# Reordering the first loads of an attention kernel, and moving its bias row out of the head

## The chip, the cores and the metric

One core of one Trainium2 chip. The metric is the device time of one execution in microseconds (us). The span of a profile, first to last instruction, is about 1.8 us shorter than the time of the same execution. In the profiles PE is TensorE (matmuls, and transposes as matmuls), DVE is VectorE; loads are issued from SP, ACT and POOL. Full and half clock mean the share of TensorE's clock that the profile records as granted.

## The reference

```python
x = A_x                                           # [1, 2048, 512] bf16
xn = layernorm(x)                                 # over 512
q = (xn @ wq) as 32 heads of 128
p = softmax(q k^T * 128**-0.5)                    # k_cache, v_cache: 32 heads, 2048 keys, 128
s = (p v) @ wo
h = relu(xn @ w1 + b1)**2                         # 512 -> 1792
g = silu(h @ w2 + b2)
out = x + s * g
```

## The kernel before

Five programs are written in one order and meet through semaphores. The query rows go through in four blocks of 512, and in each block through 32 heads. Nearly all the time is a steady loop of scores, exponentials and products, with the projections and the dense branch as side jobs in two further PSUM banks. The change concerns the head of the program: the loads of the first four x tiles, of the first head's keys (in two halves, transposed on TensorE) and of the bias row b1.

```python
    warm_up(36)                      # 36 matmuls on zeros, emitted first on TensorE
    ...
    ln_load(0, 0, SP)                # first x tile
    ln_load(0, 1, AC)                # second x tile, on ACT's queue
    load_k0(0)                       # first half of head 0's keys, SP
    fill_wq(0, AC)                   # head 0's query weights
    load_k0(1)                       # second half of the keys, SP
    ...
    k0_transpose(0); k0_copy(0)      # TensorE, then ACT
    ln_bn(0, 0); ln_rstd(0, 0, eng=DV)
    ln_bn(0, 1)
    ln_scale(0, 0)
    first_transpose(0)               # x tile 0, TensorE
    k0_transpose(1); k0_copy(1)
    ...
    first_copy(0); first_proj(0)
    bias_rows()                      # b1 transposed on TensorE
    ln_scale(0, 1)
    first_evac(0)
    bias_copy()
    first_transpose(1)
    gen_scores(0)
    ...
    second_proj(3)
    second_evac()
    t_bankF[:] = [t_q0[3], tok_xT[0][3]]   # the side banks are free
    gen_pv(3)
```

Each line emits on one engine, so an engine works in this order. The load of b1 is POOL's first DMA in this version.

The softmax here doesn't subtract the row's maximum and nothing guards it: scores larger than these inputs give would overflow.

## Time and profile before

| | kernel before |
|---|---|
| time, first three runs | 1237.77 us median (1237.75 to 1237.85) |
| span of the profile | 1236.3 us (that execution took 1238.05) |
| TensorE busy | 1231.7 us |
| first x tile landed | 3.68 us after the start of the span; the first statistics, which wait for it, start at 3.71, the prediction's figure |
| first scores start | 7.96 us |

The view of DMA issues for the first 0.9 us (tile, queue, count, size, us from issue to landing) gives the two x tiles that were issued at 0.72 (ACT) and 0.73 (SP):

```profile
x_ln<-in_A_x_dram ACTq DMA_DIRECT2D x1, 128.0 KB, 2.7
x_ln<-in_A_x_dram SPq DMA_DIRECT2D x1, 128.0 KB, 3.0
```

The reader is to see that both land within 0.3 us of each other.

### The profile page before, as it was taken

The page shows a single profiled execution, that of the slowest core. Times are in us where ns is not written, and L with a number is a line of the kernel's source. Part 1 is how long each engine was busy: PE and PEld are TensorE (multiplying, and loading weights), DVE is VectorE, ACT ScalarE, POOL GpSimd, SP SyncE. Part 2 cuts the span into 40 slices and gives each one's busy share as a digit, 9 for nine tenths or more (in the row PEclk, how much of TensorE's full clock was granted, in tenths as well). Part 3 has the DMA queues.
Part 4 walks back from the last instruction along what each step waited for, and adds up shares of the span by engine and source line. Part 5 has one row for each costly group of instructions (what it writes and reads, how often), then busy time and mean ns, then how long its engine had stood idle before and what let it go on. Part 6 is the DMA issues. An engine that isn't in the chain of part 4 may idle for free.

```text
span 1236.3 us, 26934 instructions
## 1 busy us (share of the span) xinstructions
PE 1231.7 (100%) x11885; PEld 818.8 (66%) x11885; DVE 472.8 (38%) x953; ACT 1053.5 (85%) x1044; POOL 31.9 (3%) x73
## 2 busy tenths in 40 slices
PE   9999999999999999999999999999999999999999
PEld 7666666666666666666666666666666666666665
DVE  4453323244435332334444532333344333324333
ACT  7888888888888888888888888888888888888885
POOL 1010000000002000000000200000000000000000
PEclk9999999999999999999999999999999999999999
DMA  9999998777879897778778878787788789878771
GB/s 211 203 231 209 185 178 134 130 144 143 139 152 172 141 161 129 139 139 145 133 133 170 172 138 143 141 148 134 133 146 148 146 154 158 137 134 146 145 123 31
DMA packets 686868, 185.41 MB, mean 150 GB/s; under 512 B 673536, under 2 KB 685568, under 8 KB 686752
## 3 DMA queue, kind: packets, MB, share of 16 engines
q1 hardware_dynamic: 684656, 179.62, 80.4%
q0 software_dynamic: 1424, 3.81, 1.2%
q8 instruction: 94, 1.54, 0.6%
q10 hardware_dynamic: 672, 0.26, 0.1%
q14 instruction: 22, 0.18, 0.1%
HBM read 96.60 MB, written 2.10 MB: 80 GB/s over the span
## 4 chain that ended last, share of the span: by engine, by line
PE 99%; DMA 0%; DVE 0%; issue 0%; SPq 0%; DVEq 0%
PE psO L157 38%; PE psA L152 36%; PE psF L152 25%; DMA kT<-in_A_k_cache_dram 0%; PE psA L157 0%; DVE out_t L165 0%; PE psF L196 0%; DVE tmp_t L175 0%; PE psO L196 0%; PE psO L152 0%; DVE xnT L179 0%; SPq L208 0%; PE psA L196 0%; DVEq L119 0%
## 5 line engine op out<-in xcount | busy, mean ns | idle before, releaser
L161 ACT ACTIVATE pT<-psA 128x1024 bf16<-128x1024 f32 x1024 | 1043.5, 1023 | 163.5 <-PE psA L152 118.1
L157 PEld LDWEIGHTS psO<-v_sb,pT 128*128 128x128 bf16 x8192 | 547.7, 98 | 240.5 <-issue 12.5
L157 PE MATMUL psO<-v_sb,pT 128*128 128x129 bf16 x8192 | 631.6, 220 | 0.0
L152 PE MATMUL psA<-qt_sb,kT 128*128 128x512 bf16 x2032 | 604.8, 379 | 0.0
L179 DVE COPY o_un<-psO 128x258 f32<-128x258 f32 x256 | 97.4, 422 | 399.4 <-PE psO L157 398.7
L152 PE MATMUL psF<-xnT,wq_sb 128*128 128x512 bf16 (+1 forms) x520 | 168.9, 374 | 0.2 <-DVE xnT L179 0.2
L152 PE MATMUL psF<-wo_all,oT 128*128 128x512 bf16 x480 | 163.8, 379 | 0.0
L152 PEld LDWEIGHTS psA<-qt_sb,kT 128*128 128x128 bf16 x2032 | 156.9, 98 | 0.0
L179 DVE CAST qt_sb<-psF 128x512 bf16<-128x512 f32 (+1 forms) x130 | 88.0, 677 | 97.4 <-PE psF L152 97.4
L165 DVE TENSOR_TENSOR o_bf<-o_un,rden 128x512 bf16<-128x512 f32 x128 | 88.6, 692 | 4.7 <-DVE rden L183 0.3
L152 PEld LDWEIGHTS psF<-xnT,wq_sb 128*128 128x128 bf16 x520 | 50.2, 98 | 60.1 <-issue 0.3
L171 DVE TENSOR_SCALAR r_t<-psF,b1f 128x512 bf16<-128x512 f32 x56 | 42.0, 750 | 117.5 <-PE psF L152 117.5
L152 PEld LDWEIGHTS psF<-wo_all,oT 128*128 128x128 bf16 x480 | 46.9, 98 | 56.4
L152 PE MATMUL psF<-xnT,w_sb 128*128 128x512 bf16 x224 | 77.1, 379 | 0.0
L152 PE MATMUL psF<-w_sb,h2T 128*128 128x512 bf16 x224 | 74.2, 379 | 0.0
L152 PEld LDWEIGHTS psF<-xnT,w_sb 128*128 128x128 bf16 x224 | 21.9, 98 | 26.5
L152 PEld LDWEIGHTS psF<-w_sb,h2T 128*128 128x128 bf16 x224 | 21.9, 98 | 26.5
L165 DVE TENSOR_TENSOR z_t<-psF,b2bc 128x512 f32<-128x512 f32 x16 | 11.1, 692 | 67.2 <-PE psF L152 67.2
L165 DVE TENSOR_TENSOR acc<-psF,acc 128x512 f32<-128x512 f32 x28 | 19.3, 689 | 29.9 <-PE psF L152 29.9
L208 POOL DMA_DIRECT2D out_dram<-out_t x12 | 6.7, 554 | 891.0 <-DVE out_t L165 891.0
L165 DVE TENSOR_TENSOR h2T<-r_t 128x512 bf16<-128x512 bf16 x56 | 23.8, 425 | 1.9
L183 DVE RECIPROCAL rden<-o_un 128x4 f32<-128x4 f32 x128 | 22.9, 179 | 4.4
(47 smaller groups left out, 165.6 us busy)
## 6 DMA issues: line engine op xcount, KB each, us to landing
v_sb<-in_A_v_cache_dram SPq DMA_DIRECT2D x127, 512.0 KB, 4.7
wq_sb<-in_A_wq_dram SPq DMA_DIRECT2D x127, 128.0 KB, 3.1
wo_all<-in_A_wo_dram SPq DMA_DIRECT2D x4, 1024.0 KB, 6.7
w_sb<-in_B_w_dram SPq DMA_DIRECT2D x14, 256.0 KB, 4.3
oT<-o_bf SPq DMA_TRANSPOSE x128, 4.0
x_t<-in_A_x_dram POOLq DMA_DIRECT2D x16, 128.0 KB, 3.4
kT<-in_A_k_cache_dram SPq DMA_TRANSPOSE x127, 4.5
x_ln<-in_A_x_dram SPq DMA_DIRECT2D x15, 128.0 KB, 3.8
```

The costliest lines, as they stand in the source:

```text
L152: return e.matmul(out, lhsT, rhs, start=start, stop=stop)
L157: return e.matmul(out, lhsT, rhs, start=start, stop=stop, skip_group_check=True)
L161: return e.activation(out, in_, func, bias=bias, scale=scale)
L165: return e.tensor_tensor(out, in0, in1, op)
L171: return e.tensor_scalar(out, in0, scalar1=scalar1, scalar2=scalar2, op0=op0, op1=op1)
L179: return e.tensor_copy(out, in_)
L183: return e.reciprocal(out, in_)
L208: return e.dma_start(out, in_)
```

## The change

It puts the first x tile alone at the head of SP's queue and the first half of the keys at the head of ACT's, so that both paths to the first scores start at once. It also takes the bias row out of the head: loaded from POOL later, transposed behind the last of the first projections, in a side bank instead of the scores' bank.

```diff
-    tok_b1 = S.emit_dma(GP, ...B_b1...)            # at the head of POOL's program
 ...
-                                 ... out=psA[:, 1536:1600]... deps=[tok_b1, t_ident])
+                                 ... out=bankF(1)[:, 0:64]... deps=[tok_b1, t_ident, tok_xT[0][TPB - 1]])
 ...
-                      deps=[t_k0[b], t_q0[qt], t_exp[pi - 2] if pi >= 2 else t_b1[0]],
+                      deps=[t_k0[b], t_q0[qt], t_exp[pi - 2] if pi >= 2 else None],
 ...
-    bank_no = [1]
+    bank_no = [0]
 ...
     ln_load(0, 0, SP)
-    ln_load(0, 1, AC)
-    load_k0(0)
+    ln_load(0, 1)
+    load_k0(0, AC)
     fill_wq(0, AC)
     load_k0(1)
 ...
     ln_rstd(0, 1, eng=DV)
+    tok_b1 = S.emit_dma(GP, ...B_b1...)
     first_copy(0)
     first_proj(0)
-    bias_rows()
     ln_scale(0, 1)
     first_evac(0)
-    bias_copy()
 ...
     second_evac()
-    t_bankF[:] = [t_q0[3], tok_xT[0][3]]
+    bias_rows()
+    bias_copy()
+    t_bankF[:] = [t_q0[3], t_b1[0]]
```

More of the change, by code (lines that the diff above doesn't have):

```diff
@@ L333, in bass_recurrent_scan__mha_block_cached__dense_activation_squared_relu__prompt_kernel @@
         t_ones = E(GP, partial(_memset, out=v_sb[:, i, :, Dh:Dh + 1], val=1.0))
-    tok_b1 = S.emit_dma(GP, partial(_dma, out=b1b[:], in_=B_b1.rearrange("(c p) -> c p", p=P)),
-                        sl_b1)
     t_xl = {}
@@ L394, in bass_recurrent_scan__mha_block_cached__dense_activation_squared_relu__prompt_kernel, with load_k0 @@
     t_xT = [None] * TPB
-    def load_k0(b):
+    def load_k0(b, eng=SP):
         n = NKT // 2
         t_k0[b] = S.emit_dma(
-            SP, partial(_dma, out=kT[:, NSL - 1, b * n * P:(b + 1) * n * P],
+            eng, partial(_dma, out=kT[:, NSL - 1, b * n * P:(b + 1) * n * P],
                         in_=A_k_cache[0, 0].rearrange("(p t) d -> p (t d)",
@@ L444, in bias_rows @@
     def bias_rows():
-        t_b1[0] = E(PE, partial(_peT, out=psA[:, 1536:1600].bitcast(BF16)[:, 0:NFC], in_=b1b[:],
-                                ident=ident[0:NFC, 0:NFC]), deps=[tok_b1, t_ident])
+        t_b1[0] = E(PE, partial(_peT, out=bankF(1)[:, 0:64].bitcast(BF16)[:, 0:NFC], in_=b1b[:],
+                                ident=ident[0:NFC, 0:NFC]), deps=[tok_b1, t_ident, tok_xT[0][TPB - 1]])
     def bias_copy():
         t_b1[0] = E(DV, partial(_copy, out=b1f[:],
-                                in_=psA[:, 1536:1600].bitcast(BF16)[:, 0:NFC]), deps=[t_b1[0]])
+                                in_=bankF(1)[:, 0:64].bitcast(BF16)[:, 0:NFC]), deps=[t_b1[0]])
     def first_proj(i):
@@ L913, in bass_recurrent_scan__mha_block_cached__dense_activation_squared_relu__prompt_kernel @@
     ln_rstd(0, 1, eng=DV)
+    tok_b1 = S.emit_dma(GP, partial(_dma, out=b1b[:], in_=B_b1.rearrange("(c p) -> c p", p=P)),
+                        sl_b1)
     first_copy(0)
     first_proj(0)
-    bias_rows()
     ln_scale(0, 1)
     first_evac(0)
-    bias_copy()
     first_transpose(1)
```

## The prediction

> **What bounds the kernel now.** I read the page first: the busy totals, then the chain of work that ended last, then the releasers of the costliest groups.
>
> ```profile
> PE 1231.7 (100%) x11885; PEld 818.8 (66%) x11885; DVE 472.8 (38%) x953; ACT 1053.5 (85%) x1044; POOL 31.9 (3%) x73
> PE 99%; DMA 0%; DVE 0%; issue 0%; SPq 0%; DVEq 0%
> L157 PE MATMUL psO<-v_sb,pT 128*128 128x129 bf16 x8192 | 631.6, 220 | 0.0
> L152 PE MATMUL psA<-qt_sb,kT 128*128 128x512 bf16 x2032 | 604.8, 379 | 0.0
> ```
>
> TensorE is busy for 1231.7 of the 1236.3 us of the span, it makes 99% of the chain, and both large matmul groups show 0.0 us of idle time before them. So only 4.6 us of TensorE's idle time exist in the whole execution. The change touches the start alone. The question is therefore how much earlier TensorE enters its unbroken stretch, and whether the start hands on a delay. I took the chain of waits restricted to the first 18 us, in order of time:
>
> ```profile
> 0.66 0.07 issue
> 0.73 0.40 SPq L208
> 1.12 0.06 issue
> 1.18 4.02 DMA kT<-in_A_k_cache_dram
> 5.20 0.05 issue
> 5.24 0.94 PE psO L196 x8
> 6.19 0.24 PE psF L196 x4
> 6.43 0.02 issue
> 6.45 0.43 DVE xnT L179
> 6.89 0.14 issue
> 7.02 0.38 PE psF L152 x4
> 7.41 0.11 PE psA L196
> 7.51 0.33 PE psF L196 x4
> 7.85 0.11 issue
> 7.96 1.05 PE psA L157 x16
> ```
>
> The reader is to see that the chain starts with the first half of the first head's keys (issued at 1.18, landed at 5.20), goes over their eight transposes, then over the first x tile's transposes, copy and projection, and reaches the first scores at 7.96. From there the same view is TensorE nearly without a break (one copy into xnT at 11.02 in between), up to 1232. So **the start of the first scores, 7.96, is the figure to predict**; the rest should follow it one for one.
>
> The chain names the keys, but the timeline of the first 8 us shows a second path that is nearly as long:
>
> ```profile
> 3.71 0.69 DVE L200 BATCH_NORM_STATS2 st_t<-x_ln 128x6 f32<-128x512 bf16 x1 [3.71 <-DMA x_ln<-in_A_x_dram]
> 4.72 0.68 DVE L200 BATCH_NORM_STATS2 st_t<-x_ln 128x6 f32<-128x512 bf16 x1
> 5.50 0.41 DVE L171 TENSOR_SCALAR xn_t<-x_ln,mv_t,rstd 128x512 bf16<-128x512 bf16 x1
> ```
>
> The first x tile lands at 3.71; statistics, aggregation, reciprocal root on POOL and scaling end at 5.50 + 0.41 = 5.91. Its TensorE transposes started at 6.03, when the key transposes ahead of them in TensorE's program were over. The key path therefore holds the x path back by about 0.1 us only (6.03 - 5.91, less the handing on of a semaphore). This is the number that caps what earlier keys can be worth.
>
> **What the Trainium skill says.** "DMA: Bandwidth & Descriptors", section "Issuing engines are not separate DMA queues": transfers issued from several engines run on the same 16 DMA engines and interleave, and issuing from two saves only the sequencer's issue time. The section "Queues, rings and completion order" of the same page adds that each DMA engine goes round between its queues packet by packet. The trace agrees on the sharing: between 2.2 and 2.8 us ACT's queue moved 0.09 MB and SP's 0.08 MB, both being 1024 B packets. It also shows something the sections do not say: from 1.6 to 2.2 us only ACT's queue moves anything (23 packets), though the two first loads were issued at 0.72 and 0.73. SP's first packet starts at 2.24 in the trace, ACT's at 1.76. "Trace Analysis", section "Summary: the profiler window per engine type", says that the row of such a DMA covers its issue and hides the data movement; so I use landings (0.73 + 3.0 and 0.72 + 2.7 in the view of DMA issues), not the 0.40 us rows.
>
> **The change part by part.**
>
> 1. The first half of the keys moves from second place on SP's queue (issue 1.18) to the head of ACT's (0.72). It gains 0.46 us of issue and no longer queues behind an x tile. It should start near 1.8 and has at least half of the engines: 256 KB at about two thirds of the 340 GB/s that the DMA view shows from 2.4 us on is some 1.2 us, so I estimate a landing at 3.6 to 3.9 instead of 5.20. On the path: 0.1 us, as above, because the x path stands behind it.
> 2. The second x tile moves from the head of ACT's queue to second on SP's. Landing now 0.72 + 2.7 = 3.4; then an estimated 4.0 to 4.4. VectorE wants it at 4.72, so 0.3 to 0.7 us of slack remain. On the path: 0.
> 3. The first x tile stays at the head of SP's queue, at the same issue time, but its company changes: before, 1024 B packets of the other x tile; then, 2048 B packets of keys. The mean packet times in the trace are 46 ns and 84 ns. Taking turns, x gets 1024 B each 46 + 84 = 130 ns on each of 16 engines, 126 GB/s, where it had 1024 B each 92 ns, 178 GB/s. Its 128 KB last 1.04 instead of 0.74 us at those rates, so up to 0.3 us later if ACT's queue starts first again. If instead SP starts first, x runs alone for about 0.5 us and lands up to 0.4 us earlier. This goes one for one into 7.96: between -0.4 and +0.25, and I put the mean at -0.05.
> 4. The second half of the keys and ACT's first weights: the total bytes are the same. I estimate keys at 5.0 (5.98 now, from issue and landing) and the weights at 5.9 (5.35 now). First projection 7.02 needs the weights: 1.1 us of slack. On the path: 0.
> 5. The bias transpose leaves TensorE at 7.34. It is 0.11 us of the chain, but the scores also wait for the query's copy, 7.44 + 0.29 = 7.73 on VectorE, plus about 0.2 until the weight load at 7.93. So I count at most 0.05 gained. Its copy of 0.16 us on VectorE leaves a stretch that isn't on the chain: 0.
> 6. The bias transpose comes back on TensorE after the last second projection, near 14.7, where TensorE is continuous: one 128x14 matmul with its weight load, 0.06 to 0.1 us. The bias row now leaves POOL near 6.9 and needs 4.6 us (the landing of that load before), so it lands near 11.5, 3 us ahead of its use. Its copy, 0.16 us, follows the query's copy at 15.45 and delays the first o_un copy to about 15.6, while head 1's products need that bank at 17.67. On the path: +0.08.
> 7. The side banks start with the other parity (0 instead of 1). The comparison of the two programs shows 12 lines of difference on TensorE, all of them the bias transpose's place, so no job moves. 0.
>
> Sum: -0.1 (1) - 0.05 (3) - 0.05 (5) + 0.08 (6) = **-0.12 us**, of 1237.77, that is 0.01%.
>
> **The rivals.**
>
> The keys really gate, as the chain says. Then 1.3 to 1.6 us of earlier keys would be worth about that much, 1236.3. Against it stands the x path, at 5.91 before any key matters, so I give it little.
>
> The x tile slows down. If the 2048 B packets take turns at the head of the row, the first scores start at 8.1 to 8.2, and the time is 1237.9 to 1238.0. For it: ACT's queue began 0.5 us ahead of SP's in the trace. Against it: which of two issues 0.01 us apart is served first may swap.
>
> A new wait: the second x tile too late for VectorE's second statistics, which stand ahead of the first scaling in VectorE's program. It would have to land after 4.72, against my 4.4; then the time grows by the excess, 0.1 to 0.3 us. Or the bias row lands after 14.7; each us late would stop TensorE for a us. With 3 us of slack I rule that out.
>
> Hidden anyway: everything is swallowed later. TensorE has no idle time to swallow it in, so a shift of the first scores stays in the total, either way.
>
> **Range and chances.** Every case lies between -1.5 and +0.4 us; the likely ones between -0.6 and +0.3. The repeats of before spread by 0.1 us. So 1237.6, with 1237.0 to 1238.1 as the range. Two per cent are 24.8 us, five times all the idle time that TensorE has: within 2% has 0.985, and what is left covers a surprise of state or hardware that the profile does not show.
>
> **What would show it.** In the chain after: the first scores' start near 7.85 (7.5 to 8.2) instead of 7.96, with the x tile's load, statistics and scaling at its head in place of the keys. In the timeline: key transposes near 3.9 instead of 5.24, the first statistics between 3.3 and 4.0, the second before 4.8. The bias matmul near 14.7 with no idle time ahead of it. TensorE's busy time within 0.2 us of 1231.7 apart from the start. I would be wrong if TensorE shows a new idle stretch after 8 us, if the first weights land after 7, or if the scores start 1 us or more earlier, which would mean that the x path was not what held them.

## The result, and the profile after

| | before | changed |
|---|---|---|
| time, median of 6 | 1237.78 us (1237.74 to 1238.13) | 1239.38 us (1238.77 to 1240.30) |
| ratio | | 1.0013 (95%: 1.0000 to 1.0026) |
| span of the profile | 1236.3 | 1237.0 (the fastest of the six, 1238.77) |
| first x tile landed | 3.68 | 4.30 |
| first scores start | 7.96 | 8.45 |

Ratios are the mean time of one kernel's fast runs over that of the other's of the same rounds, so not quite the ratio of the medians. The changed kernel is about 1.6 us slower in the median, and its times spread over 1.5 us where those of before spread over 0.4. (Of all 42 runs of before, two are outliers, at 1238.77 and 1239.49.) The chain of waits at the start of the changed kernel, in order of time (start, us, what):

```profile
0.73 3.58 DMA x_ln<-in_A_x_dram
4.30 0.02 issue
4.33 0.70 DVE st_t L200
...
6.11 0.42 DVE xn_t L171
6.54 0.05 issue
6.58 0.41 PE psF L196 x4
...
7.59 0.38 PE psF L152 x4
7.97 0.37 PE psF L196 x4
8.34 0.11 issue
8.45 1.05 PE psA L157 x16
```

The keys have left the chain, as they should, and the x path has taken their place. But it got longer at its first link: the load that landed at 3.68 lands at 4.30. The DMA issues of the first 0.9 us show the pair that now goes first:

```profile
kT<-in_A_k_cache_dram ACTq DMA_DIRECT2D x1, 256.0 KB, 3.8
x_ln<-in_A_x_dram SPq DMA_DIRECT2D x1, 128.0 KB, 3.6
```

The keys landed at 0.72 + 3.8 = 4.5 instead of 5.20, and TensorE had transposed them by 5.85. Then it waited for x (the timeline, TensorE alone; in brackets the idle time before, and what ended it):

```profile
6.58 0.40 PE L196 MATMUL psF<-ident,xn_t 128*128 128x128 bf16 x4 [0.73 <-DVE xn_t L171]
```

A second loss stands further on in the chain. First the stretch of the kernel before, then that of the changed one:

```profile
14.50 0.22 PE psO L152 x4
14.72 0.45 PE psO L157 x8
15.17 0.89 PE psA L157 x16
```

```profile
14.98 0.22 PE psO L152 x4
15.21 0.11 PE psF L196
15.32 0.56 PE psO L157 x8
15.88 0.89 PE psA L157 x16
```

From the last second projection to the next scores it is 15.17 - 14.50 = 0.67 us before and 15.88 - 14.98 = 0.90 after: in the chain the bias transpose takes 0.11 us and the product behind it 0.11 more. The two losses are (8.45 - 7.96) + 0.2 = 0.7 us, the whole difference of the two spans. TensorE's busy time on the page (1221.0 against 1231.7) must not be read as idle time: the page counts 11678 matmuls instead of 11885, so 207 records are missing, while all 11885 weight loads are there.

This profile caught the fastest run of six. What made the others slower it cannot tell.

### The profile page after: what moved, and what is told of

It is laid out like the page before. It is cut to its first block, busy times and chain, and to the rows that moved or that the text cites. A ratio compares the mean times of both kernels' runs of the same rounds, so it can differ in the third digit from the quotient of the medians.

```text
span 1237.0 us, 26728 instructions
## 1 busy us (share of the span) xinstructions
PE 1221.0 (99%) x11678; PEld 819.4 (66%) x11885; DVE 472.8 (38%) x953; ACT 1054.6 (85%) x1044; POOL 32.0 (3%) x73
## 4 chain that ended last, share of the span: by engine, by line
PE 98%; issue 1%; DVE 0%; DMA 0%; POOL 0%; DVEq 0%
PE psO L157 38%; PE psA L152 35%; PE psF L152 25%; DMA x_ln<-in_A_x_dram 0%; PE psA L157 0%; DVE out_t L165 0%; PE psF L196 0%; DVE tmp_t L175 0%; PE psO L152 0%; DVE xnT L179 0%; DVE st_t L200 0%; POOL rstd L165 0%; DVE xn_t L171 0%; DVE mv_t L204 0%; DVE ve_t L171 0%
## 5 line engine op out<-in xcount | busy, mean ns | idle before, releaser
L161 ACT ACTIVATE pT<-psA 128x1024 bf16<-128x1024 f32 x1024 | 1044.5, 1024 | 162.9 <-PE psA L152 117.6
L152 PE MATMUL psA<-qt_sb,kT 128*128 128x512 bf16 x1840 | 562.9, 379 | 10.1
L152 PE MATMUL psF<-xnT,wq_sb 128*128 128x512 bf16 (+1 forms) x508 | 165.7, 374 | 0.4 <-DVE xnT L179 0.2
```

Source lines behind the costliest of these rows:

```text
L152: return e.matmul(out, lhsT, rhs, start=start, stop=stop)
L161: return e.activation(out, in_, func, bias=bias, scale=scale)
```

## The experiments

The theories. **K**: key packets beside the first x tile hold it up, so it lands late. **B**: the bias move is the cost. **C**: TensorE's idle stretch ahead of the x transposes makes it miss a window in which its full clock is released. Every kernel ran five times, with runs of the kernel before on the same chip between them, and gave one profile, which falls on the first of the five. The experiments went in four groups, on three chips; compare first within a group (the median of before is given where it changes). All results were correct.

**The changed kernel again.** No edit.

> The changed kernel once more, for its spread (it ran from 1238.77 to 1240.30 us, the kernel before from 1237.74 to 1238.13) and a second profile. Theory K (key packets that stall a DMA engine hold up the first x tile behind them): x lands late again, at another time than 4.31 us (4.0 to 5.5), and the first scores' start moves with it one for one; time 1238.7 to 1240.3. Theory C (TensorE's clock: the idle stretch ahead of the x transposes delays the release of the full clock): x lands at 4.3 again and the excess over the profiled 1238.77 is a later or broken clock.

1238.96 us median (1238.51 to 1240.24), before 1237.93 (1237.78 to 1238.35). x landed at 4.47, the scores started at 8.62. The loss and the spread repeat; this profile is a middle run. Its group has queues_only, bias_only and fill_gap as well.

**The reordered loads alone.**

```diff
 (kernel before)
-    ln_load(0, 1, AC)
-    load_k0(0)
+    ln_load(0, 1)
+    load_k0(0, AC)
```

> The kernel before with the reordered loads alone (both first x tiles on SP, first half of the keys at the head of ACT's queue), bias row as before. Theory K and C both: all of the spread and most of the loss, 1238.4 to 1240; first statistics at 4.3 or later instead of 3.71. Rival B (the bias move is the cost): like before, 1237.8.

1238.65 us (1238.27 to 1239.21). x landed at 4.27, scores at 8.51. That is 0.72 us above before, of 1.03 for the changed kernel in the same group. Most of the loss comes with the loads; B falls as the main cause.

**The bias move alone.** The changed kernel with those two lines as before.

> The kernel before with the bias row's later load and later transpose alone, loads as before. Theory K and C: 1237.9 to 1238.1, that is the 0.2 us that the chain of the changed kernel shows around the late bias transpose (0.11 us for it and 0.11 us longer product behind it), less up to 0.1 us at 7.4; spread 0.1 us as before. Rival B: 1238.7 to 1240.

1238.08 us (1237.86 to 1238.41), 0.15 above the median of before. x landed at 3.42. Against the changed kernel only the order of the loads differs, and the head start of SP's queue is the same (its first packet came 0.16 us ahead of ACT's in both profiles): so it is the loads that move x, by 0.9 us between these two profiles. In this one the second half of the keys landed late, at 6.72, and set the scores.

**Eight matmuls in the idle stretch.**

```diff
 (changed kernel)
     ln_scale(0, 0)
+    warm_up(8)
     first_transpose(0)
```

> The changed kernel with 8 more warm-up matmuls between the key transposes and the x transposes, in TensorE's idle stretch of 0.73 us. Theory C: the clock is released as early as before (5.96 us after the start of the span, not 6.47), the spread shrinks to 0.1 to 0.3 us and the time falls by 0.3 to 1.5 us against the changed kernel of the same rounds. Theory K: x lands as late as in the changed kernel, time and spread within 0.3 us of it.

1238.65 us (1238.50 to 1238.86), x at 4.13, scores at 8.28. Time and spread fell as C has it, but x also happened to land 0.2 to 0.3 us earlier than in the two profiles of the changed kernel, so this alone does not decide.

**The weights, not the keys, at the head of ACT's queue.**

```diff
 (changed kernel)
-    load_k0(0, AC)
     fill_wq(0, AC)
+    load_k0(0, AC)
```

> The changed kernel with ACT's two loads swapped: first head's weights (256 B packets) at the head, first half of the keys (2048 B packets) behind them. Theory K (key packets beside the first x tile hold it up): x lands at 3.2 to 3.6 instead of 4.13 to 4.47, the first scores wait for the keys again (landing 5.0 to 5.5), start 7.9 to 8.1, time 1238.0 to 1238.3, spread under 0.5. Rival (x lands late because the second x tile is on its own queue or because both queues start at once): x at 4.1 to 4.5 as in the changed kernel, time 1238.5 to 1240.

1238.36 us (1238.23 to 1238.63), before 1237.95. x landed at 3.37, though the second x tile was still behind it on SP's queue and both queues were in use. So it is the keys beside x that make it late. One rival is that x had SP's queue alone for longer here (ACT's first packet came 0.54 us after SP's); it cannot be the whole, because after_26 below, with 0.33 us of head start, has x at 4.23, and bias_only, with 0.16, at 3.42. The keys landed at 5.94, later than expected, and the scores at 8.30 wait for them: with the keys away, x is early and the keys are late.

**Fewer warm-up matmuls, in the kernel before.**

```diff
-    warm_up(36)
+    warm_up(26)
```

> The kernel before with 26 instead of 36 warm-up matmuls, so TensorE idles from about 3.9 until the keys' transposes at 5.24, loads untouched. Theory C (an idle stretch there lets TensorE miss a clock window, at a phase that differs from run to run): some runs 1 to 2 us longer, spread over 1 us, like the changed kernel's tail at 1240.2. Theory K alone: 1237.8 to 1238.4, spread as before; the transposes at the lower clock may add 0.1 to 0.4.

The five times were 1239.10, 1237.74, 1238.82, 1237.77 and 1238.97: two groups. The profile is of the slowest. x and the keys landed no later than before (3.40 and 5.12), but TensorE stood idle ahead of the key transposes:

```profile
5.16 1.03 PE L196 MATMUL psO<-ident,kT 128*128 128x128 bf16 x8 [1.22 <-DMA kT<-in_A_k_cache_dram]
```

The clock's record shows the full clock only from 10.00 us (5.96 in the kernel before), and the transposes, projection and scores ahead of it ran at the slower rate. The times say that such an idle stretch cost over 1 us in three runs and nothing in two; only one of them was profiled. C's mechanism is real.

**The reordered loads alone, with the eight matmuls.** queues_only and fill_gap together.

> The reordered loads alone (as in queues_only) with the 8 matmuls of fill_gap in TensorE's idle stretch; bias row as before. If the idle stretch makes the tail: spread under 0.4, median 1238.2 to 1238.6 (fill_gap less 0.2 for the late bias transpose). If the landings alone make it: as queues_only, 1238.3 to 1239.2.

1239.01 us (1238.42 to 1239.22), before 1237.95: no better than queues_only, and the spread is 0.8, not under 0.4. That is the outcome for the landings alone. Filling the stretch does not lower the median.

**Keys in smaller rows.** The first half of the keys in two loads of 1024 B rows (changed kernel, load_k0):

```diff
-        ...one load of [128 partitions x 8 x 128]
+        for s in range(2 if b == 0 else 1):     # two loads of [128 x 4 x 128] on one semaphore
```

> The changed kernel with the first half of the keys as two loads of 1024 B rows instead of one of 2048 B rows, both still at the head of ACT's queue. If turn-taking by packet makes x late (84 ns key packets between 46 ns x packets, 8 per engine): x lands about 8 x 38 ns = 0.3 us earlier, 3.8 to 4.1, time 0.3 less than the changed kernel (1238.6). If single key packets that take 0.5 to 1.3 us hold up x on one engine: x at 4.1 to 4.5 as before the edit, time unchanged, 1238.5 to 1240.2.

1238.55 us (1238.18 to 1238.83), before 1237.94. x landed at 3.66, 0.4 us or more earlier than in any profile with 2048 B key rows. So how the keys are cut matters; whether it is the row or the load, which is also half as long, one profile does not tell. The head start of SP's queue was 0.35 us, much as in after_26 (0.33), where x landed at 4.23. The gain is larger than the 0.3 us of the packet sum. The four x transposes took 0.61 us (0.41 in the changed kernel), which gave part of it back; a slow clock fits that, but this profile holds no record of the clock.

**The changed kernel with fewer warm-up matmuls**, 26 for 36.

> The changed kernel with 26 instead of 36 warm-up matmuls: a second idle stretch ahead of the one it has. Theory C: most runs miss a clock window; two groups as in short_warm but with a larger step, about 1238.7 and 1240.0 to 1241, most of them in the upper one, and the profile of an upper one shows the full clock from about 8.5 us or later and first scores at 9 or later. Without the clock: as the changed kernel, 1238.5 to 1239.0, with at most 0.4 for the slower transposes.

1240.47 us (1239.59 to 1241.19), before 1237.94; all five above the changed kernel's median. x landed at 4.23, the scores started at 8.58, with idle stretches of 0.62 and 1.41 us ahead. The stretches of the profile (length; busy us and instructions by engine; granted clock; DMA share; GB/s) show a half-clock window:

```profile
3.50:7.00 3.50, 1.46 (x22) 1.12 (x20) 2.34 (x8) 1.02 (x1) 0.76 (x2) 1.00 1.12 317
7.00:10.50 3.50, 3.45 (x34) 2.95 (x32) 2.09 (x6) 1.90 (x2) 1.80 (x4) 0.51 1.29 228
10.50:14.00 3.50, 3.43 (x61) 3.25 (x59) 2.27 (x8) 2.95 (x4) 0.95 (x3) 1.00 1.19 240
```

TensorE was busy for 1.46 of 3.50 us in the first row, and for the next 3.413 us (7.04 to 10.46 in the clock's record) it got half the clock (column before the last two).

**The changed kernel twice more, to catch an upper run.** No edit.

> The changed kernel a third time, for its upper runs (5 of 11 so far above 1239.2). If the missed clock window makes them: 1 to 3 of 5 runs above 1239.2, and a profile that falls on one shows half clock, or first scores that take 1.6 to 1.9 us instead of 1.05. If only late landings make them: a profile of an upper one shows x at 4.8 or later with score matmuls of 1.05 us.

> The same kernel and the same expectation as after_third; a further profile and five further times.

1239.39 us (1238.48 to 1240.48) and 1239.28 us (1238.59 to 1240.77), before 1237.80. The first profile is an upper run, 1240.23. Its chain of waits:

```profile
0.73 4.11 DMA x_ln<-in_A_x_dram
...
7.12 0.61 PE psF L196 x4
7.73 0.85 PE psO L196 x8
8.58 0.43 PE psF L152 x4
9.01 0.43 PE psF L196 x4
9.43 0.05 issue
9.48 1.49 PE psA L157 x16
```

It has both: x landed at 4.83, 0.5 us later than in the first profile, and the clock's record shows the full clock only from 10.43. The four x transposes last 0.61 instead of 0.41 us and the 16 score matmuls 1.49 instead of 1.05. Against the first profile the scores start 1.03 us later, 0.52 of it by the landing, and the scores themselves lose 0.44; with 0.5 us of clock ahead of the scores that makes the 1.4 us by which the spans differ (1238.4 and 1237.0). The other profile (1239.13) has x at 4.66 and the full clock: a late landing alone.

**The changed kernel without an idle stretch**, 44 warm-up matmuls for 36.

> The changed kernel with 44 instead of 36 warm-up matmuls, so that TensorE is busy until the key transposes end at about 6.2 to 6.6 and the idle stretch ahead of the x transposes is gone. Theory C: no run above 1239.2, median 1238.5 to 1238.9. Without the clock: as the changed kernel, about two runs of five above 1239.2.

1239.20 us (1238.68 to 1239.43): by its test this went against C, with two runs above 1239.2, as many as expected without the clock, and a median above C's range. The median stays. Only with a line drawn afterwards, at 1239.5, are the upper runs gone: of 21 runs of the changed kernel six lie above it, of the 15 runs with the stretch filled (fill_gap, queues_fill, after_44) none does. But queues_only, whose stretch of 0.70 us is not filled, has none in five either. So the counts alone do not show that the clock makes the upper runs.

Two other things do more. Each run's result lists its mean granted clock: 0.999 in four of the six upper runs, 1.000 in the 15 others of the changed kernel, in all 15 filled ones and in the 36 runs of before that list it. In those four a stretch at a lower clock was recorded (the profile of after_26, with one such stretch, gives 0.9986; where it lay, the result does not say). A late first release, as in after_third, does not show in this mean.

And the clock records of 16 profiles can be put side by side (small_keys has none). In 13 the full clock lasts 1232.211 us; in short_warm and after_third it lasts 1228.798, which is 3.413 less; in after_26 it is on for 3.413, off for 3.413, then on for 1228.798. So it changes on a grid of 3.413 us, which lies elsewhere in each run (the full clock first comes between 3.63 and 6.61 us in the 14 profiles that are not late). Counted back along the grid from the first full clock, every step in which TensorE idled for up to 0.77 us (time ahead of the first matmul included) was followed by the full clock, and none with 0.79 us or more was (the profile models where matmuls end, so take this line as rough). Once full, the clock outlived up to 1.52 us of idle in a step at the start (keys_after_wq) and was lost after 2.04 (after_26). That is why the changed kernel's first profile, with 0.61 us idle in its step, lost nothing, after_third with 0.98 lost a whole step, and after_again, idle for 1.15 us but at the full clock since 5.18, lost nothing either.

**Two tries to beat the kernel before.** The first leaves the x tiles as they were and moves the weights out of the keys' way:

```diff
 (kernel before)
     load_k0(0)
-    fill_wq(0, AC)
-    load_k0(1)
+    load_k0(1, AC)
+    fill_wq(0)
```

> A try to beat the kernel before: its x loads and first keys stay (x on SP and ACT, first keys behind the first x on SP), the second half of the keys goes to ACT behind the second x tile, and the first head's weights go to SP behind the first keys. Theory K: the x tiles have only x beside them, so x lands at 3.4 to 3.7; the keys no longer share with 256 B packets, landing near 4.7 to 5.0 instead of 5.20; then the x path alone sets the first scores, 7.85 to 7.95, time 1237.7 to 1237.9, at most 0.1 faster. It loses if the weights land after 7.0.

> The best try once more: 1237.7 to 1237.9, within 0.2 us of the kernel before; if it is really 0.1 to 0.2 faster, its median lies below that of before again.

1237.79 us (1237.71 to 1238.16), before 1237.95; and 1237.73 (1237.68 to 1237.75), before 1237.80. Ratios 0.9999 and 0.9998 with intervals of 0.13% to both sides: no slower, and whether it is faster by the 0.07 to 0.16 us of the medians is not settled. x landed at 3.43 and 3.40, the keys at 4.74 and 4.77, the scores started at 7.66 and 7.63, and none of its ten runs was a slow outlier. The chain of wq_later no longer starts with a load:

```profile
0.98 4.02 PE psA L152 x36
5.00 0.84 PE psO L196 x8
5.85 0.28 PE psF L196 x4
```

The 36 warm-up matmuls end at 5.00, after the keys' landing, and hold the transposes up. So here a still earlier landing of keys or x has little left to give.

The second cuts the first x tile into two loads of 64 partitions at the heads of both queues:

```diff
 (wq_later)
-    ln_load(0, 0, SP)
-    ln_load(0, 1, AC)
+    for eng, lo, hi in ((SP, 0, 64), (AC, 64, 128)): ...   # halves of x tile 0
+    ln_load(0, 1, AC)
```

> A try to beat the kernel before: wq_later with the first x tile cut in two loads of 64 partitions at the heads of both queues, second x tile behind on ACT. If company at the head decides, x lands at 2.9 to 3.2 instead of 3.43, and the first scores come at 7.3 to 7.6 instead of 7.66; time 1237.5 to 1237.75. If the cost of a load is in its start and landing and not in its company, x lands at 3.4 and the time stays at 1237.8.

1239.19 us (1238.77 to 1241.49): a miss. x landed at 3.30, 0.1 us earlier, but the second x tile only at 5.41, and VectorE waited 1.01 us for it; the second half of the keys, issued on ACT behind two x loads at 2.23, landed at 7.21 and set the scores, 8.66.

**All profiles side by side.** The last column is the span less the start of the first scores:

| kernel | beside the first x tile | x landed | scores start | span | rest |
|---|---|---|---|---|---|
| before | x, 1024 B | 3.68 | 7.96 | 1236.3 | 1228.3 |
| wq_later | x | 3.43 | 7.66 | 1236.0 | 1228.3 |
| wq_later_again | x | 3.40 | 7.63 | 1235.9 | 1228.3 |
| x_halves | its other half, 1024 B | 3.30 (both) | 8.66 | 1237.0 | 1228.3 |
| queues_only | keys, 2048 B | 4.27 | 8.51 | 1236.8 | 1228.3 |
| queues_fill | keys | 4.09 | 8.32 | 1236.6 | 1228.3 |
| bias_only, bias late | x | 3.42 | 8.09 | 1236.6 | 1228.5 |
| changed, bias late | keys | 4.30 | 8.45 | 1237.0 | 1228.5 |
| after_again, bias late | keys | 4.47 | 8.62 | 1237.2 | 1228.5 |
| after_fourth, bias late | keys | 4.66 | 8.81 | 1237.3 | 1228.5 |
| fill_gap, bias late | keys | 4.13 | 8.28 | 1236.8 | 1228.5 |
| after_44, bias late | keys | 4.22 | 8.37 | 1236.9 | 1228.5 |
| keys_after_wq, bias late | weights, 256 B | 3.37 | 8.30 | 1236.8 | 1228.5 |
| small_keys, bias late | keys, 1024 B | 3.66 | 8.02 | 1236.6 | 1228.5 |
| short_warm, clock late | x | 3.40 | 8.46 | 1237.3 | 1228.85 |
| after_third, bias late, clock late | keys | 4.83 | 9.48 | 1238.4 | 1228.95 |
| after_26, bias late, clock lost | keys | 4.23 | 8.58 | 1237.8 | 1229.22 |

The rest is a constant: 1228.3 us with the bias early, 1228.5 with it late, and 0.4 to 0.7 more where the scores themselves ran at the lower clock. So everything else is decided before the first scores. With 2048 B key rows beside it x never landed before 4.09, without them never after 3.68.

## Why the prediction was wrong

The time stayed within 2% of before, as forecast, but came out above the range (1237.0 to 1238.1): 1239.38.

*What bounds the kernel.* Right: the first scores' start passes into the total one for one, as the table's last column shows, and the x path stood just behind the keys.

*Step 1, earlier keys.* The mechanism was right and the gain on the path too (about 0); the landing was 4.51, not 3.6 to 3.9. My own figures, a start at 1.8 and 1.2 us of moving, add up to 3.0; for the 0.6 to 0.9 on top I gave no source.

*Step 2, second x tile.* It landed at 4.90, later than my 4.0 to 4.4; since VectorE's second statistics moved to 5.34 with x, nothing waited. Step 4 held on the path: the weights landed at 5.30. The second half of the keys came at 6.11, not 5.0, but its transposes stand behind those of x (6.58).

*Step 3, the first x tile: the step that failed.* It said "This goes one for one into 7.96: between -0.4 and +0.25, and I put the mean at -0.05." The first half is right, the size wrong. SP's queue even started first (1.76, ACT's 1.92), the case that I counted as a gain, and x landed 0.6 us later; over all profiles it is 0.4 to 1.4 us over the landings with x beside it (4.09 to 4.83 against 3.40 to 3.68). The rival "The x tile slows down" named the event, with scores at 8.1 to 8.2, and tied it to ACT's queue starting first; they came at 8.45 with SP's first. The step was a sum of packet times over equal engines. Its 84 ns is the median of the 256 key packets in that trace; their mean is 96. But a load has landed only when its slowest DMA engine is done. In the changed kernel's first profile the fastest engine had x at 3.15 and the slowest at 4.30; before, it was 3.28 and 3.68. Single packets that started ahead of x's landing took far longer than the mean: up to 1264 ns there (a key packet) and 1675 ns in after_fourth (an x packet), against 244 ns in the profile of before. What makes such packets long is open, and that they are the cause of the late landing is not shown: packets of 555 ns in bias_only and 673 ns in keys_after_wq stand in profiles where x landed early all the same. Shown is only that the keys beside x make it late.

*Step 5 and 6, the bias.* I wrote "On the path: +0.08" for the late transpose; it measured 0.2, because the product behind it grew by as much as the transpose itself took. Its absence at 7.4 gained 0.08 to 0.09, not 0.05: from x's landing to the first scores it is 4.15 us in the five profiles with these loads, the bias late and the full clock in time (the changed kernel, after_again, after_fourth, fill_gap, after_44), and 4.24 and 4.23 in queues_only and queues_fill, which have the same loads and the bias early. The move costs about 0.13 us in all, near the 0.15 of bias_only.

*Missing altogether: the clock.* The prediction never asked what an idle TensorE does at this point. I listed waits as rivals, not the rate at which TensorE would run after one. A lower clock is on record in five of the six upper runs (above 1239.5, of 21): one profile with a late full clock, and four results with a mean clock of 0.999. The sixth (1240.24, mean 1.000) stays open, and so does how much of each upper run is clock and how much landing. The clock does not make the median. The three signs that I named for being wrong (a new idle stretch after 8 us, weights after 7, scores 1 us earlier) did not occur in the changed kernel's first profile: none of them watched for a late x tile or a slow clock.

In sum, in the two profiles of before and changed: x landed 0.62 us later, of which 0.04 did not count, because before the keys held the x path back by that much; the bias gave 0.09 at the head and took 0.22 later. That is 0.7 us, the difference of the spans (1237.0 and 1236.3). Between the medians (1239.28 of all 21 runs of the changed kernel, 1237.92 of all 42 of before) it is 1.4 us. No profile of the changed kernel at the full clock fell on a run above its median. An estimate from the table (time less 1.8, less 1228.5, less 4.15): such a median run has x at about 4.8, inside the range seen. In six runs of 21, clock and perhaps landing add 0.7 to 1.5 us to that.

## What to carry to other kernels

The transfer that heads the critical path lands with its slowest engine (4.30 here, the fastest 3.15), so look at what stands beside it and measure the landing over several runs; a sum of typical packet times was too low here. An earlier arrival on one path is worth nothing if it takes from the path right behind it, and a TensorE that it leaves idle near the start may also lose clock, at a phase that differs from run to run. A small instruction moved into a continuous stretch cost its own time (0.11 us) and as much again in its neighbour.

## What the Trainium skill lacked or had wrong

- "DMA: Bandwidth & Descriptors", section "Issuing engines are not separate DMA queues": it says that issuing from several engines saves only issue time. It lacks that the company at a queue's head moves a single load's landing: the same x tile landed at 3.40 to 3.68 us beside another x tile, 3.37 beside 256 B rows (one profile), 3.66 beside keys in two loads of 1024 B rows (one profile) and 4.09 to 4.83 beside keys in 2048 B rows.
- The same page, section "Queues, rings and completion order": it has each DMA engine take turns between its queues by packet. Its packets hold several descriptors, while the profile's are single rows; the prediction took them for the same, and no run here tells. The 0.3 us that it worked out so fit the fastest engine: from SP's first packet to that engine's landing it took 1.39 us (1.76 to 3.15), and 1.04 before (2.24 to 3.28). The section gives no packet times, so it lacks the spread that decides the slowest: most packets took 46 or 84 ns, single ones up to 1264 and 1675.
- "TensorE: Matmul & The Clock Gate", section "HAM oscillation — how this bites in real kernels": it gives as the rule to avoid idle gaps over about 3.4 us. Here much shorter gaps sufficed: with gaps of 0.62 and 1.41 us TensorE fell back to half clock for 3.413 us (after_26). Elsewhere the page tells of frequent short idles that did the same in one kernel, without a length. It does not say how much idle a step may hold: here 0.77 us still let the full clock come and 0.79 did not; once full it outlived 1.52 and was lost after 2.04. The length of the step agrees with the 3413 ns of the same page's section "What's actually happening".
